# Transposing attention exponentials by DMA as two float16 values, in a kernel of attention, an FFN and a soft mixture of experts

## The chip, the cores and the metric

The kernel runs on one core of a Trainium2 chip. The metric is the device time of one execution in microseconds (us). The engines are PE (TensorE, which multiplies matrices), DVE (VectorE), ACT (ScalarE), POOL (GpSimd) and SP (SyncE, which here only issues DMAs). Each engine runs its own instructions in the order in which they were written. PE writes its results to PSUM, and another engine must move them from there.

## The reference

```python
# attention: 4 batches, 8 heads, 576 tokens, head size 64
scores = q @ k.T / 8
thresh = max(scores) - tau
scores = where(scores >= thresh, scores, -1e9)
attn = exp(scores - max(scores)); attn /= attn.sum() + 1e-9
x = (attn @ v), heads side by side             # 2304 tokens x 512
# FFN
g = relu(x @ w_in)**2                          # 512 -> 2048
x = g @ w_out                                  # 2048 -> 512
# soft mixture of experts: 8 experts with 4 slots each
logits = x @ phi
d = softmax(logits, over tokens); slot_input = d.T @ x
slot_out[e] = relu(slot_input[e] @ w1[e]) @ w2[e]
out = softmax(logits, over slots) @ slot_out
```

All is float32.

## The kernel before, in words

**Attention.** A job is a pair of heads of one batch; there are 16 pairs. A pair has five query tiles. Tiles j = 0 to 3 hold 128 queries of both heads; tile 4 ("mixed") holds the last 64 queries of each head. For each tile PE computes the scores into three PSUM banks (`s_mm`). For each head DVE scales them and takes the row maximum (`top`, line 442), POOL adds tau to that (`bound`, 448), ACT takes the exponentials (`expo`, 455), and DVE zeroes those under the threshold and sums the rest (`keep`, 459). The result e of a tile has 128 rows and 2 x 576 columns. The product with v contracts over keys, so e has to be transposed: PE does it in nine blocks of 128 x 128 (`turn`; the transposes stand under the helper's line 239), and ACT copies them out of PSUM into the tile pt (`evac`, 496 and 498).

**Groups.** Tiles 0 and 1 form group 0, tiles 2 and 3 group 1, and tile 4 group 2. Once a group's two tiles are transposed, PE multiplies v with pt (`av`: line 547 for each head, writing one half of the output's partitions, and 536 for the last 64 keys of both heads), and DVE multiplies by the reciprocal sums and writes the FFN's input xp (560). So an xp tile holds a unit of 256 tokens: one batch and one group, of all four head pairs. There are three buffers of xp.

**FFN and experts.** Nine units of 256 tokens go through the FFN. Its float32 products are split into high and low parts in the format float32r, three one-pass products each: 192 products for a unit (line 830). Before that, 32 chunks of weights are converted (`conv_ops`). w_out is folded into phi, so the logits come from the FFN's hidden layer (645). The end (`tail`) loads the expert weights into the buffers that come free.

**What sets the order.** A planner (`Plan`) simulates the engines at build time with a cost, a key (priority) and dependences for each step, and emits the instructions in the order that it finds. The engines then keep that order. Attention steps have keys by job, FFN steps on PE have keys behind all of them (`FKEY`), so that the FFN's products fill the gaps. Buffers are slots of a tag: `acq` takes one, `rel` gives it back. SP's DMAs share one modelled bus; the figure `dma=` is what a transfer holds it. A negative one (`turn`) also keeps SP busy until shortly before the transfer's end.

```python
self.bus = max(self.bus, self.now + DMA_LEAD) + o.dma
o.end = max(self.bus, o.end + DMA_LEAD) + DMA_TAIL
if o.turn:
    self.free[o.eng] = max(self.now + o.cost, self.bus - DMA_TAIL)
```

Of the kernel before, what the change touches and what calls it, by code (L numbers as in the profile page):

```python
# [9 lines left out]
F32 = mybir.dt.float32  # L10
F32R = mybir.dt.float32r
F16 = mybir.dt.float16
# [127 lines left out]
def tile_kernel(  # L140
# [34 lines left out]
    EB = 3  # L175
# [1 line left out]
    PTB = 2  # L177
    XPB = 3
    MMB = 4
    QKB = 3  # L180
    WAIT = 0.0
    DQ = 2.212
    T0 = 20.0
# [16 lines left out]
    state = {}  # L200
    plan = Plan(
        dict(
            s=1, ma=1, mm=MMB, u=UB, e=EB, em=1, pt=PTB, ptm=1, rp=3, rb=3, rr=3, xp=XPB, xh=2, xl=1, gt=MC // 2 + 1,
            gk=GB, l4=1, dT=1, qt=QKB, kt=QKB, vraw=2, vbd=2,
            sm=5, raw64=RB, cv=CB, wt=2,
        ),
        ("mm", "ma"),
        WAIT,
        DQ,
    )  # L210
# [1 line left out]
    def add(kind, eng, cost, fn, deps=(), key=0.0, *args, **kw):  # L212
        return plan.add(eng, cost, fn, deps, key + LEAD.get(kind, 0.0), *args, **kw)
# [6 lines left out]
    stack_f = const.tile([128, 128], F32, name="stack_f")  # L220
    stack_i = stack_f[:, 0:NS]
    tau_sb = const.tile([128, 1], F32, name="tau_sb")
    tau_p = const.tile([128, 1], F32, name="tau_p")
    nscale = const.tile([128, 1], F32, name="nscale")
    wphi = const.tile([128, MC, NS], F32, name="wphi")
# [14 lines left out]

    def setup():
        make_identity(nc, sg[:, 0:128])
        nc.vector.tensor_copy(ident_r, sg[:, 0:128])
        nc.sync.dma_start(out=tau_sb, in_=tau.partition_broadcast(128))
        nc.vector.tensor_scalar(tau_p, tau_sb, 0.0, None, ALU.max)
        nc.vector.tensor_scalar(nscale, tau_sb, 0.0, -SCALE, ALU.is_ge, ALU.mult)
        nc.vector.tensor_reduce(stack_i, ident.rearrange("p (g s) -> p s g", s=NS), AX.X, ALU.add)
        for g in range(1, NG):
            nc.vector.tensor_copy(stack_f[:, NS * g:NS * g + NS], stack_i)
# [100 lines left out]
    def attn_ops():  # L350

        at, ac = state["at"], state["ac"]
        vbd = [ac.tile([128, NP, 192], F32, name=f"vbd{i}") for i in range(2)]
        for t in vbd:
# [10 lines left out]

        def key(p, x):
            return begins[p] + x  # L370

        def prep(x):
            p, b, n, h0 = x, jobs[x][0] // NP, jobs[x][0] % NP, 2 * (jobs[x][0] % NP)
            d = P[x]
            k0 = key(x - 1, 2.0) if x else 0.0
            ld = {}
            if n == 0 and b not in last:
                def lvrem():
                    y = v[b, :, 512:S, :].rearrange("(n h) p d -> p n h d", h=2)
                    for a, r0, c0 in ((0, 0, 0), (1, 64, 64), (1, 0, 128)):  # L380
                        nc.sync.dma_start(out=vbd[b % 2][r0:r0 + 64, :, c0:c0 + 64], in_=y[:, :, a, :])
                last[b] = add("lrem", "SP", 1.9, lvrem, [], k0 - 4, ["vbd"], dma=1.1)
            for nm in "kqv":
                def lraw(nm=nm):
                    if nm == "v":
                        t = raw[p, nm] = at.tile([128, 2, 4 * D], F32, tag=nm + "raw", name="raw", bufs=2)
                        nc.sync.dma_start(
                            out=t, in_=v[b, h0:h0 + 2, 0:512, :].rearrange("h (r j) d -> r h (j d)", j=4)
                        )
                        return  # L390
                    t = d[nm + "t"] = at.tile([128, SQ], F32, tag=nm + "t", name=nm + "t", bufs=QKB)
                    nc.sync.dma_start(out=t, in_=src[nm][b, n])
                ld[nm] = add("lraw", "SP", 0.6, lraw, [], k0 - (5 if nm != "v" else 2), [nm + ("raw" if nm == "v" else "t")],
                             dma=0.73 if nm == "v" else 0.95)
            d["v_op"], d["vr_op"], d["q_op"], d["k_op"] = ld["v"], last[b], ld["q"], ld["k"]
            d["v"], d["vb"] = (lambda: raw[p, "v"]), vbd[b % 2][:, n, :]
            d["ready"] = [ld["q"], ld["k"]]

        def tiles(p):
            d = P[p]  # L400
# [4 lines left out]
            def tile_ops(n, j):  # L405
# [27 lines left out]
                for a in heads:  # L433
                    c = 0 if mixed else 2 * a + j % 2
                    k = key(p, n * TA + a * TA / 2)

                    def top(a=a, c=c):
                        if "sm" not in gd:
                            gd["sm"] = at.tile([128, 16], F32, tag="sm", name="sm", bufs=5)
                        u = o["u", a] = at.tile([128, S], F32, tag="u", name="u", bufs=UB)  # L440
                        s0 = 960 * a
                        nc.vector.tensor_scalar(  # L442
                            u, o["s"][:, s0:s0 + S], nscale, None, ALU.mult, ALU.min, accum_out=gd["sm"][:, c:c + 1]
                        )

                    def bound(c=c):
                        sm = gd["sm"]
                        nc.gpsimd.tensor_scalar(sm[:, 4 + c:5 + c], sm[:, c:c + 1], tau_p, None, ALU.add)  # L448

                    def expo(a=a, c=c):  # L450
                        if "e" not in o:
                            w = S if mixed else 2 * S
                            o["e"] = at.tile([128, w], F32, tag="em" if mixed else "e", name="e", bufs=1 if mixed else EB)
                        e = o["e"][:, a * S:(a + 1) * S]
                        nc.scalar.activation(e, o["u", a], AF.Exp, scale=-1.0, bias=gd["sm"][:, c:c + 1])  # L455

                    def keep(a=a, c=c):
                        sm, e = gd["sm"], o["e"][:, a * S:(a + 1) * S]
                        nc.vector.scalar_tensor_tensor(  # L459
                            e, o["u", a], sm[:, 4 + c:5 + c], e, ALU.is_le, ALU.mult, accum_out=sm[:, 8 + c:9 + c]  # L460
                        )

                    X = add("top", "DVE", 0.89, top, [S_], k, ["u"] + (["sm"] if first_g and not a else []), [("s", S_)])
                    if first_g and not a:
                        gd["first"] = X
                    h = add("bound", "POOL", 0.52, bound, [X], k)
                    E_ = add("expo", "ACT", 0.77, expo, [X] + ([ee] if a else []), k, [] if a else ["em" if mixed else "e"])
                    if not a:
                        ee = E_
                    K_ = add("keep", "DVE", 0.92, keep, [E_, h], k, rel=[("u", X)])  # L470
                    gd.setdefault("keep", []).append(K_)
                    ks.append(K_)

                def turn(x):
                    o["p", x] = mm_tile()
# [10 lines left out]

                def evac(x):
                    if "pt" not in gd:
                        w = 1 if mixed else 2
                        gd["pt"] = at.tile(  # L490
                            [128, 5 if mixed else 9, w, 128], F32, tag="ptm" if mixed else "pt", name="pt", bufs=1 if mixed else PTB
                        )
                    pt, i = gd["pt"], 0 if mixed else j % 2
                    if x == 2:
                        r, m = (slice(0, 64), 4) if mixed else (slice(0, 128), 8)
# [1 line left out]
                    else:  # L497
                        nc.scalar.activation(pt[:, 4 * x:4 * x + 4, i], o["p", x].rearrange("p (c s) -> p c s", c=4), AF.Copy)  # L498

                tag = "em" if mixed else "e"  # L500
                pk = "ptm" if mixed else "pt"
                for x in heads + (2,):
                    k = key(p, n * TA + min(x, 1) * TA / 2)
                    dep = ks if x == 2 else [ks[x]]
# [6 lines left out]
            def group_ops(g, n):  # L511
# [17 lines left out]
                def av(lo, hi):  # L529
# [4 lines left out]
                    for m in range(lo, hi):  # L534
# [5 lines left out]
                        for a in range(2):  # L540
# [4 lines left out]
                            else:  # L545
                                lt, rh = vr[:, a, m * D:(m + 1) * D], pt[:, 4 * a + m].rearrange("p t s -> p (t s)")
                            nc.tensor.matmul(po[i, :n_], lt, rh, start=m == 0, stop=m == 4)  # L547
                def evac():
                    if g == 2:
                        for a in range(2):  # L550
# [5 lines left out]
                    else:  # L556
                        if kk == 0:
                            xp[b, g] = fx.tile([128, KC, NU], F32, tag="xp", name="xp", bufs=XPB)
                        o = xp[b, g][:, kk, :]
                    nc.vector.tensor_tensor(o, gd["po"][:, 0:256], gd["rr"], ALU.mult)  # L560

                if g < 2:
                    rc = add("spread", "POOL", 0.6, spread, [rc], k, ["rb"], [("rp", rc)])
# [5 lines left out]
                        transpose(gd["ro"][:, 128 * t:128 * t + 128], y)  # L569

                def revac():
                    gd["rr"] = at.tile([128, 256], F32, tag="rr", name="rr", bufs=3)
                    n = 128 if g == 2 else 256
                    nc.scalar.activation(gd["rr"][:, 0:n], gd["ro"][:, 0:n], AF.Copy)

# [2 lines left out]
                rc = add("r_evac", "ACT", 0.3 if g == 2 else 0.4, revac, [rt], k, [], [("mm", rt)])  # L578
                deps = gd["turn"] + [d["v_op"], d["vr_op"]]
                first = None  # L580
                for lo, hi_ in ((0, 5),) if g == 2 else ((0, 2), (2, 5)):
                    c = (hi_ - lo) * (0.51 if g < 2 else 0.3) 
                    rel = []
                    if hi_ == 5:
                        rel = [("ptm" if g == 2 else "pt", gd["pto"])]
                    o = add("av", "PE", c, lambda lo=lo, hi_=hi_: av(lo, hi_), deps, k, [] if lo else ["ma"], rel)
                    first = first or o
                    deps = [o]
                rel = [("ma", first), ("rr", rt)]
                ev = add("evac", "DVE", 0.25 if g == 2 else 0.45, evac, [o, rc], k, ["xp"] if g < 2 and kk == 0 else [], rel)  # L590
                ev_at.setdefault("rem" if g == 2 else (b, g), []).append(ev)
                att.append(ev)
# [548 lines left out]
```

## Time and profile before

| What | Value |
|---|---|
| Median of 3 runs | 738.61 us (738.5 to 738.76) |
| The profiled execution's own time | 741.05 us |
| Its span, first to last instruction | 739.2 us |
| Busy: PE, DVE, ACT, POOL | 674.4, 423.7, 373.4, 133.6 us |
| Mean granted TensorE clock | 0.974 of full speed |
| Attention's writes of xp | from 41.0 us to 503.6 us |
| FFN products | from 159.0 us to 661 us |

A row of a group of instructions reads: line, engine, operation, tile written <- tiles read, shape, count | busy us together, mean ns of one | idle time of the engine just ahead of them and what ended it. The mean of a matmul is its latency: matmuls are pipelined, so what one takes from PE is the distance to the next one's start. A timeline row gives start, length, engine, line, and how many equal instructions were merged. A row of DMA issues ends with the KB of one and the us from issue to landing. PEld is PE's weight load, SPq is SP's queue.

### The profile page before, as it was taken

How to read it: one execution, taken by the hardware profiler on the slowest of the kernel's cores; microseconds unless marked ns; L12 is line 12 of the kernel's file. 1: busy time of each engine (PE TensorE's matmuls, PEld its weight loads, DVE VectorE, ACT ScalarE, POOL GpSimd, SP SyncE). 2: the span in 40 equal slices, each digit the busy share in tenths (PEclk: the TensorE clock that was granted, in tenths of full speed). 3: DMA queues.
4: the chain of work that ended last, by engine and by line, in shares of the span. 5: the costliest groups of instructions: out<-in, count | busy, mean ns of one | idle time of the engine just before them, and what ended most of it. 6: DMA issues, size and time to landing. Idle time of an engine off the chain costs nothing.

```text
span 739.2 us, 13383 instructions
## 1 busy us (share of the span) xinstructions
PE 674.4 (91%) x5198; PEld 489.8 (66%) x5198; DVE 423.7 (57%) x1110; ACT 373.4 (51%) x726; POOL 133.6 (18%) x236
## 2 busy tenths in 40 slices
PE   1677899999999999999999999999999999998873
PEld 0333666767676766877678769767988979794312
DVE  6999978876677668746677571572323140413403
ACT  4776766765666556537566543654333333332203
POOL 4876433210211111111012100010000000000000
PEclk9888979999999999999999999999999999999998
DMA  7955857311110210010110000105900000197986
GB/s 229 305 167 178 264 166 247 110 45 51 36 52 16 61 37 4 34 51 30 47 36 6 1 1 1 30 1 184 397 4 30 1 30 1 59 367 277 388 319 255
DMA packets 38959, 83.50 MB, mean 113 GB/s; under 512 B 6641, under 2 KB 11761, under 8 KB 38897
## 3 DMA queue, kind: packets, MB, share of 16 engines
q1 hardware_dynamic: 38896, 82.65, 32.8%
q8 instruction: 41, 0.67, 0.4%
q14 instruction: 22, 0.17, 0.1%
HBM read 73.73 MB, written 8.91 MB: 112 GB/s over the span
## 4 chain that ended last, share of the span: by engine, by line
PE 79%; DVE 8%; DMA 4%; ACT 4%; issue 2%; POOL 1%; SPq 1%; DVEq 0%; ACTq 0%; POOLq 0%
PE mm L830 29%; PE mm L239 16%; PE po L547 9%; PE s L426 8%; PE mm L759 2%; PE mm L645 2%; PE po L536 2%; DMA w<-in_moe_w_dram 2%; PE mm L961 2%; PE s L421 2%; DVE raw L286 1%; PE s L415 1%; DVE cv L290 1%; DVE e L459 1%; PE mm L332 1%
## 5 line engine op out<-in xcount | busy, mean ns | idle before, releaser
L830 PE MATMUL mm<-xh,w 128*128 128x256 f32 x1152 | 166.4, 287 | 0.0
L830 PEld LDWEIGHTS mm<-xh,w 128*128 128x128 f32 x1152 | 147.6, 191 | 13.7 <-issue 11.0
L459 DVE SCALAR_TENSOR_TENSOR e<-u,sm,e 128x576 f32<-128x576 f32 x144 | 122.7, 862 | 35.0 <-ACT e L455 32.9
L442 DVE TENSOR_SCALAR_CACHE_REDUCE u<-s,nscale 128x576 f32<-128x576 f32 x144 | 114.5, 811 | 49.2 <-PE s L426 40.9
L455 ACT ACTIVATE e<-u,sm 128x576 f32<-128x576 f32 x144 | 110.0, 779 | 32.1 <-DVE u L442 31.4
L498 ACT ACTIVATE pt<-mm 128x512 f32<-128x512 f32 x144 | 82.8, 597 | 55.1 <-PE mm L239 54.8
L836 ACT ACTIVATE gt<-mm 128x512 f32<-128x512 f32 x72 | 43.0, 597 | 125.8 <-PE mm L830 124.8
L448 POOL TENSOR_SCALAR sm<-sm,tau_p 128x1 f32<-128x1 f32 x144 | 53.1, 369 | 287.9 <-DVE u L442 228.9
L239 PE MATMUL mm<-ident_r,e 128*128 128x128 f32 (+1 forms) x656 | 98.0, 286 | 5.6 <-DVE e L459 5.6
L239 PEld LDWEIGHTS mm<-ident_r,e 128*128 128x128 f32 (+1 forms) x656 | 76.5, 146 | 33.4 <-DVE e L459 12.6
L830 PE MATMUL mm<-xl,w 128*128 128x256 f32 x576 | 92.5, 283 | 0.0
L547 PE MATMUL po<-pt,raw 128*64 128x256 f32 (+1 forms) x768 | 79.0, 342 | 0.9 <-DVE xp L560 0.9
L830 PEld LDWEIGHTS mm<-xl,w 128*128 128x128 f32 x576 | 79.3, 192 | 0.0
L426 PE MATMUL s<-kt,qt 64*128 64x512 f32 x256 | 77.0, 680 | 0.0
L547 PEld LDWEIGHTS po<-pt,raw 128*64 128x64 f32 x768 | 44.6, 140 | 29.2 <-issue 10.7
L421 PE MATMUL s<-kt,qt 128*128 128x128 f32 x128 | 27.3, 297 | 29.4 <-DMA qt<-in_q_dram 11.9
L842 DVE SCALAR_TENSOR_TENSOR gt<-mm,gt 128x512 f32<-128x512 f32 x18 | 12.4, 691 | 67.7 <-ACT gt L836 67.5
L421 PEld LDWEIGHTS s<-kt,qt 128*128 128x128 f32 x128 | 20.7, 201 | 33.7 <-issue 19.8
L239 PEld LDWEIGHTS mm<-ident_r,gt 128*128 128x128 f32 x288 | 31.7, 143 | 11.2 <-issue 8.2
L239 PE MATMUL mm<-ident_r,gt 128*128 128x128 f32 x288 | 38.7, 278 | 0.3 <-ACT pt L498 0.2
L844 ACT ACTIVATE gt<-gt 128x512 f32<-128x512 f32 x54 | 34.0, 630 | 1.4
L801 POOL TENSOR_TENSOR xl<-xp,xh 128x256 fp32r<-128x256 f32 x16 | 12.3, 780 | 115.9 <-PE mm L830 82.6
(126 smaller groups left out, 742.0 us busy)
## 6 DMA issues: line engine op xcount, KB each, us to landing
w<-in_moe_w_dram SPq DMA_DIRECT2D x25, 1024.0 KB, 11.9
raw<-in_moe_w_in_dram SPq DMA_DIRECT2D x16, 512.0 KB, 4.4
raw<-in_moe_w_out_dram SPq DMA_DIRECT2D x16, 512.0 KB, 4.2
kt<-in_k_dram SPq DMA_DIRECT2D x20, 320.0 KB, 3.1
qt<-in_q_dram SPq DMA_DIRECT2D x20, 320.0 KB, 4.0
raw<-in_v_dram SPq DMA_DIRECT2D x20, 256.0 KB, 2.8
w_out<-cv SPq DMA_DIRECT2D x16, 256.0 KB, 4.8
w<-w_out SPq DMA_DIRECT2D x4, 1024.0 KB, 9.8
```

What stands on the lines that cost most here:

```text
L239: nc.tensor.transpose(out_, in_, ident[:n, :n])
L421: nc.tensor.matmul(s[:, 1].rearrange("p (c s) -> p c s", s=64)[:, 0:8:7], lt, d["kt"][:, 512:SQ], start=True, stop=True)
L426: nc.tensor.matmul(s[:, 2 * a], lt[i], d["kt"][i, 0:512], start=True, stop=True)
L442: nc.vector.tensor_scalar(u, o["s"][:, s0:s0 + S], nscale, None, ALU.mult, ALU.min, accum_out=gd["sm"][:, c:c + 1])
L448: nc.gpsimd.tensor_scalar(sm[:, 4 + c:5 + c], sm[:, c:c + 1], tau_p, None, ALU.add)
L455: nc.scalar.activation(e, o["u", a], AF.Exp, scale=-1.0, bias=gd["sm"][:, c:c + 1])
L459: nc.vector.scalar_tensor_tensor(e, o["u", a], sm[:, 4 + c:5 + c], e, ALU.is_le, ALU.mult, accum_out=sm[:, 8 + c:9 + c])
L498: nc.scalar.activation(pt[:, 4 * x:4 * x + 4, i], o["p", x].rearrange("p (c s) -> p c s", c=4), AF.Copy)
L547: nc.tensor.matmul(po[i, :n_], lt, rh, start=m == 0, stop=m == 4)
L830: nc.tensor.matmul(o["h"][:, i * NU:(i + 1) * NU], a, c, start=n_ == 0, stop=n_ == len(terms) - 1)
L836: nc.scalar.activation(g, o["h"], AF.Relu)
L844: nc.scalar.activation(g, g, AF.Square)
```

## The change

For 18 groups (in batches 2 to 4: group 1 of every head pair, and group 0 of every second one) the transposes leave PE:

- e is split into two float16 values, a high part (ACT, `high`) and the remainder (POOL, `low`), side by side in a tile hl of 128 x 2304.
- One DMA from SP (`dturn`) transposes that tile from SBUF to SBUF, 18 blocks of 128 x 128. PE's transposes and ACT's evacuations of these tiles go.
- v is also split into two float16 parts, once for each head pair that has such a group (`split_v`). A power of two scales v into range; it comes from the sum of absolute values (two ACT passes with a sum, two one-column PE products, four short DVE steps). Then ACT makes the high part and DVE the low one.
- The product becomes three one-pass float16 products (`av_split`): high with high, low v with high e, and high v with low e. The scale is undone when DVE writes xp.
- For space: k and q have two buffers instead of three, rr two instead of three, and the mixed tiles take their e and pt buffers from the common ones. The planner hands out xp slots to whichever step comes first.

```diff
-    QKB = 3
+    QKB = 2
+    HB = 2
...
-            s=1, ma=1, mm=MMB, u=UB, e=EB, em=1, pt=PTB, ptm=1, rp=3, rb=3, rr=3, xp=XPB, xh=2, xl=1, gt=MC // 2 + 1,
+            s=1, ma=1, mm=MMB, u=UB, e=EB, pt=PTB, rp=3, rb=3, rr=2, hl=HB, vh=1, mx=2, xp=XPB, xh=2, xl=1, gt=MC // 2 + 1,
...
-        ("mm", "ma"),
+        ("mm", "ma", "xp"),
...
+        def by_dma(p, g):
+            b, n = jobs[p][0] // NP, jobs[p][0] % NP
+            return g < 2 and (b > 0 and (g == 1 or n % 2 == 1))
...
+        def split_v(x):
+            p, d, k0 = x, P[x], key(x, 0.0)
+            def absum():
+                mx = d["mx"] = at.tile([128, 16], F32, tag="mx", name="mx", bufs=2)
+                d["vh"] = at.tile([128, 2, 640], F16, tag="vh", name="vh", bufs=1)
+                main = d["v"]().rearrange("p h d -> p (h d)")
+                nc.scalar.activation(d["vh"][:, 0, 0:512], main, AF.Abs, accum_out=mx[:, 0:1])
+                nc.scalar.activation(d["vh"][:, 1, 0:128], d["vb"][:, 0:128], AF.Abs, accum_out=mx[:, 1:2])
+            def stats():
+                d["ps"] = mm_tile()
+                for i in range(2):
+                    nc.tensor.matmul(
+                        d["ps"][:, 0:1], ones.to_broadcast([128, 128]), d["mx"][:, i:i + 1], start=i == 0, stop=i == 1
+                    )
+            def scales():
...
+            def hi():
+                for t, y in parts():
+                    nc.scalar.activation(t[:, 0], y, AF.Copy, scale=d["mx"][:, 8:9])
+            def lo():
+                for t, y in parts():
+                    nc.vector.scalar_tensor_tensor(t[:, 1], y, d["mx"][:, 8:9], t[:, 0], ALU.mult, ALU.subtract)
+            ab = add("v_abs", "ACT", 0.9, absum, [d["v_op"], d["vr_op"]], k0, ["mx", "vh"])
+            st = add("v_sum", "PE", 0.4, stats, [ab], k0, ["mm"])
+            sc = add("v_scale", "DVE", 0.5, scales, [st], k0, rel=[("mm", st)])
+            h = add("v_hi", "ACT", 0.9, hi, [sc], k0)
+            d["vs_op"], d["vs_ready"] = ab, add("v_lo", "DVE", 0.95, lo, [h], k0)
...
+                def high(a):
+                    if not a:
+                        o["hl"] = at.tile([128, 4 * S], F16, tag="hl", name="hl", bufs=HB)
+                    nc.scalar.activation(o["hl"][:, a * S:(a + 1) * S], o["e"][:, a * S:(a + 1) * S], AF.Copy)
+                def low(a):
+                    c = slice(a * S, (a + 1) * S)
+                    nc.gpsimd.tensor_tensor(
+                        o["hl"][:, (2 + a) * S:(3 + a) * S], o["e"][:, c], o["hl"][:, c], ALU.subtract
+                    )
+                def dturn():
+                    if "pt" not in gd:
+                        gd["pt"] = at.tile([128, 2, 18, 128], F16, tag="pt", name="pt", bufs=PTB)
+                    nc.sync.dma_start_transpose(out=gd["pt"][:, j % 2], in_=o["hl"])
+                if by_dma(p, g) and not mixed:
+                    ls = []
+                    for a in heads:
+                        k = key(p, n * TA + a * TA / 2)
+                        h = add("high", "ACT", 0.68, lambda a=a: high(a), [ks[a]] + ([hl] if a else []), k, [] if a else ["hl"])
+                        hl = hl if a else h
+                        ls.append(add("low", "POOL", 1.72, lambda a=a: low(a), [h], k, rel=[("e", ee)]))
+                    k = key(p, n * TA + TA / 2)
+                    t = add("dturn", "SP", 3.0, dturn, ls, k, [] if "pto" in gd else ["pt"], [("hl", hl)], dma=-6.8)
+                    gd.setdefault("pto", t)
+                    gd.setdefault("turn", []).append(t)
+                    return
...
+                def av_split():
+                    po = gd["po"] = ma.tile([128, 512], F32, tag="ma", name="po", bufs=1)
+                    terms = ((0, 0), (1, 0), (0, 9))
+                    for i, (y, c) in enumerate(terms):
+                        for m in range(4):
+                            for a in range(2):
+                                c0 = 256 * a + m * D
+                                nc.tensor.matmul(
+                                    po[64 * a:64 * a + 64, :n_], d["vh"][:, y, c0:c0 + D], gd["pt"][:, :, c + 5 * a + m, :],
+                                    start=i == 0 and m == 0, stop=False,
+                                )
+                    for i, (y, c) in enumerate(terms):
+                        nc.tensor.matmul(
+                            po[:, :n_], d["vh"][:, y, 512:640], gd["pt"][:, :, c + 4, :], start=False, stop=i == 2
+                        )
...
+                if by_dma(p, g):
+                    o = first = add("av", "PE", 1.9, av_split, deps + [d["vs_ready"]], k, ["ma"],
+                                    [("pt", gd["pto"]), ("vh", d["vs_op"])])
```

More of the change, by code (lines that the diff above doesn't have):

```diff
@@ L222, in tile_kernel @@
     tau_sb = const.tile([128, 1], F32, name="tau_sb")
+    ones = const.tile([128, 1], F32, name="ones")
     tau_p = const.tile([128, 1], F32, name="tau_p")
@@ L242, in setup @@
         make_identity(nc, sg[:, 0:128])
+        nc.vector.memset(ones, 1.0)
         nc.vector.tensor_copy(ident_r, sg[:, 0:128])
@@ L397, in prep, with parts @@
             d["ready"] = [ld["q"], ld["k"]]
+            if any(by_dma(x, j // 2) for j in jobs[x][1] if j < 4):
+                split_v(x)
+        def split_v(x):
[13 more added lines that the diff above has]
+            def scales():
+                mx = d["mx"]
+                e, f = mx[:, 4:5], mx[:, 8:9]
+                nc.vector.tensor_scalar(e, d["ps"][:, 0:1], 2.0**-40, None, ALU.max)
+                nc.vector.tensor_scalar(e.bitcast(I32), e.bitcast(I32), 0x7F800000, None, ALU.bitwise_and)
+                nc.vector.tensor_scalar(f.bitcast(I32), e.bitcast(I32), -1.0, 268.0 * 2**23, ALU.mult, ALU.add)
+                nc.vector.tensor_scalar(mx[:, 12:13], e, 2.0**-14, None, ALU.mult)
+            def parts():
+                v = d["v"]().rearrange("p h d -> p (h d)")
+                return (d["vh"][:, :, 0:512], v), (d["vh"][:, :, 512:640], d["vb"][:, 0:128])
+            def hi():
[9 more added lines that the diff above has]
+            d["vs_op"], d["vs_ready"] = ab, add("v_lo", "DVE", 0.95, lo, [h], k0)
+            plan.release(d["vs_ready"], [("vraw", d["v_op"]), ("vbd", d["vr_op"])])
@@ L451, in expo @@
                         if "e" not in o:
-                            w = S if mixed else 2 * S
-                            o["e"] = at.tile([128, w], F32, tag="em" if mixed else "e", name="e", bufs=1 if mixed else EB)
+                            o["e"] = at.tile([128, 2 * S], F32, tag="e", name="e", bufs=EB)
                         e = o["e"][:, a * S:(a + 1) * S]
@@ L466, in tile_ops @@
                     h = add("bound", "POOL", 0.52, bound, [X], k)
-                    E_ = add("expo", "ACT", 0.77, expo, [X] + ([ee] if a else []), k, [] if a else ["em" if mixed else "e"])
+                    E_ = add("expo", "ACT", 0.77, expo, [X] + ([ee] if a else []), k, [] if a else ["e"])
                     if not a:
@@ L488, in evac @@
                     if "pt" not in gd:
[L489 to L492, printed above, removed]
+                        gd["pt"] = at.tile([128, 9, 2, 128], F32, tag="pt", name="pt", bufs=PTB)
                     pt, i = gd["pt"], 0 if mixed else j % 2
@@ L498, in evac @@
                         nc.scalar.activation(pt[:, 4 * x:4 * x + 4, i], o["p", x].rearrange("p (c s) -> p c s", c=4), AF.Copy)
-                tag = "em" if mixed else "e"
-                pk = "ptm" if mixed else "pt"
+                tag, pk = "e", "pt"
                 for x in heads + (2,):
@@ L559, in evac @@
                         o = xp[b, g][:, kk, :]
-                    nc.vector.tensor_tensor(o, gd["po"][:, 0:256], gd["rr"], ALU.mult)
+                    if by_dma(p, g):
+                        nc.vector.scalar_tensor_tensor(o, gd["po"][:, 0:256], d["mx"][:, 12:13], gd["rr"], ALU.mult, ALU.mult)
+                    else:
+                        nc.vector.tensor_tensor(o, gd["po"][:, 0:256], gd["rr"], ALU.mult)
                 if g < 2:
@@ L571, in revac @@
                 def revac():
-                    gd["rr"] = at.tile([128, 256], F32, tag="rr", name="rr", bufs=3)
+                    gd["rr"] = at.tile([128, 256], F32, tag="rr", name="rr", bufs=2)
                     n = 128 if g == 2 else 256
@@ L580, in group_ops @@
                 first = None
-                for lo, hi_ in ((0, 5),) if g == 2 else ((0, 2), (2, 5)):
+                if by_dma(p, g):
+                    o = first = add("av", "PE", 1.9, av_split, deps + [d["vs_ready"]], k, ["ma"],
+                                    [("pt", gd["pto"]), ("vh", d["vs_op"])])
+                for lo, hi_ in () if by_dma(p, g) else ((0, 5),) if g == 2 else ((0, 2), (2, 5)):
                     c = (hi_ - lo) * (0.51 if g < 2 else 0.3)
@@ L584, in group_ops @@
                     if hi_ == 5:
-                        rel = [("ptm" if g == 2 else "pt", gd["pto"])]
+                        rel = [("pt", gd["pto"])]
                     o = add("av", "PE", c, lambda lo=lo, hi_=hi_: av(lo, hi_), deps, k, [] if lo else ["ma"], rel)
@@ L588, in group_ops @@
                     deps = [o]
-                rel = [("ma", first), ("rr", rt)]
+                rel = [("ma", first), ("rr", rt)] + ([("mx", d["vs_op"])] if by_dma(p, g) else [])
                 ev = add("evac", "DVE", 0.25 if g == 2 else 0.45, evac, [o, rc], k, ["xp"] if g < 2 and kk == 0 else [], rel)
```

## The prediction

> **What bounds the kernel now.** First the page's busy shares and slices, then busy times by stretch.
>
> ```profile
> PE 674.4 (91%) x5198; PEld 489.8 (66%) x5198; DVE 423.7 (57%) x1110; ACT 373.4 (51%) x726; POOL 133.6 (18%) x236
> PE   1677899999999999999999999999999999998873
> ```
> ```profile
> 20.00:80.00 60.00, 43.67 (x208) 26.01 (x210) 59.37 (x117) 41.97 (x78) 42.15 (x43) 0.83 0.69 222
> 140.00:500.00 360.00, 356.58 (x2782) 258.97 (x2782) 232.95 (x668) 205.80 (x414) 52.47 (x144) 1.00 0.10 31
> ...
> 506.00:661.00 155.00, 153.60 (x1318) 137.55 (x1319) 40.06 (x102) 56.34 (x105) 5.74 (x8) 1.00 0.32 118
> 661.00:740.00 79.00, 56.72 (x453) 24.14 (x451) 24.50 (x66) 16.31 (x33) 1.90 (x2) 0.95 0.84 309
> ```
>
> The columns are window, length, then busy us of PE, its weight loads, DVE, ACT, POOL, then granted clock, DMA share, GB/s. From 20 to 80 us DVE is the bound (59.4 of 60). From 140 to 661 PE is (356.6 of 360, then 153.6 of 155); DVE is at 65% there, DMA at 0.10. The end after 661 is set by weight loads (DMA 0.84). So time taken from PE between 140 and 500, where batches 2 to 4 run their attention, shortens the kernel as long as PE finds other work. That other work is the FFN: the attention's writes to the xp tiles show how both are tied.
>
> ```profile
> 154.00 0.42 DVE L560 TENSOR_TENSOR xp<-po,rr 128x256 f32<-128x256 f32 x1 [0.24 <-PE po L536]
> ...
> 261.08 0.42 DVE L560 TENSOR_TENSOR xp<-po,rr 128x256 f32<-128x256 f32 x1
> ...
> 324.30 0.28 DVE L795 CAST xh<-xp 128x256 fp32r<-128x256 f32 x1
> 324.50 0.41 DVE L560 TENSOR_TENSOR xp<-po,rr 128x256 f32<-128x256 f32 x1
> ...
> 417.96 0.28 DVE L795 CAST xh<-xp 128x256 fp32r<-128x256 f32 x1
> 418.16 0.41 DVE L560 TENSOR_TENSOR xp<-po,rr 128x256 f32<-128x256 f32 x1
> ...
> 503.57 0.42 DVE L560 TENSOR_TENSOR xp<-po,rr 128x256 f32<-128x256 f32 x1 [1.91 <-PE po L536]
> ```
>
> Between 261 and 324 no attention output is written: the first one of batch 3's second unit comes right behind the read (L795) that frees an xp tile, and so again at 418. The attention waits for FFN units, and FFN for PE. Faster PE therefore also moves the attention forward.
>
> **The change part by part.** A "group" is two 128-row tiles of a head pair; 18 groups, 36 tiles, take the new path.
>
> ```profile
> 250.03 1.20 PE L239 MATMUL mm<-ident_r,e 128*128 128x128 f32 x9
> ...
> 250.99 1.19 PE L830 MATMUL mm<-xh,w 128*128 128x256 f32 x8
> ...
> 257.76 1.95 PE L547 MATMUL po<-pt,raw 128*64 128x256 f32 x16
> ...
> 259.64 0.70 PE L536 MATMUL po<-pt,vbd 128*128 128x256 f32 x2
> ...
> 260.18 0.38 PE L239 MATMUL mm<-ident_r,rb 128*128 128x128 f32 x2
> ```
> ```profile
> 443.13 17.46 PE mm L830 x144
> ```
> ```profile
> L704 PE MATMUL mm<-al,stack_f 32*128 32x1 f32 x16 | 2.9, 250 | 0.0
> ```
>
> *Removed from PE.* Nine transposes of a tile hold PE from 250.03 to 250.99, the next start: 0.96 us. Two tiles: 1.92 us per group. The float32 product with v lasts from 257.76 to 260.18: 2.42 us. Together 4.34.
>
> *Added to PE.* 27 products of 256 columns: 24 write half of the output's partitions and 3 write all. No float16 product is in the trace. The nearest row is the FFN's one-pass product of the same 256 columns, 17.46/144 = 0.121 us. If the two heads' products run side by side, as the float32 ones do (16 records, two for each of 8 products, in 1.88 us: 0.47 for a pair, near four passes of 0.121), there are 12 + 3 slots: 1.82 us. If they don't, 27 slots: 3.27 us. I take 1.82, since the float32 rows show the pairing. Saved: 2.52 us per group, 45.4 us in 18; low end 1.07 per group, 19 us.
>
> The sum over v's partitions adds two one-column products for each of 12 head pairs. L704's 16 records are eight products, 2.9/8 = 0.36 us each; 24 of them cost 8.7 us. PE net: 45.4 - 8.7 = 36.7 us (ends 10.6, and 45.4 if the sums fall into gaps).
>
> ```profile
> L459 DVE SCALAR_TENSOR_TENSOR e<-u,sm,e 128x576 f32<-128x576 f32 x111 | 89.6, 817 | 31.9 <-ACT e L455 30.1 <-POOL sm L448 1.2
> ...
> L498 ACT ACTIVATE pt<-mm 128x512 f32<-128x512 f32 x112 | 64.3, 598 | 43.4 <-PE mm L239 43.2
> ...
> L844 ACT ACTIVATE gt<-gt 128x512 f32<-128x512 f32 x24 | 15.1, 628 | 0.5
> ...
> L496 ACT ACTIVATE pt<-mm 128x128 f32<-128x128 f32 x50 | 14.1, 281 | 5.6 <-PE mm L239 5.6
> ```
> ```profile
> L299 POOL TENSOR_TENSOR cv<-cv,raw 128x512 f32<-128x512 f32 x16 | 23.8, 1488 | 18.9 <-DVE cv L290 9.1 <-ACT raw L294 5.2 <-DMA raw<-in_moe_w_out_dram 3.5
> ```
> ```profile
> L459 DVE SCALAR_TENSOR_TENSOR e<-u,sm,e 128x576 f32<-128x576 f32 x16 | 17.2, 1085 | 0.5 <-ACT e L455 0.5
> ```
>
> *ACT.* Evacuations go: 36 x (2 x 0.598 + 0.281) = 53 us. The float16 halves come: 72 x 0.628 x 576/512 = 51 us; v's magnitude and high part, 12 x 2 x (0.628 + 0.281) = 22 us. 206 becomes 226 of some 345 us (the 360 less part of the gain): beside PE.
>
> *POOL.* The low halves are 72 x 1.488 x 576/512 = 121 us, so POOL goes from 52 to 173 us. It isn't full, but its other steps (L448, which L459 waits for) queue behind a 1.67 us instruction.
>
> *DVE.* v's low parts, 12 x 0.817 x 640/576 = 11 us; four one-column steps for each pair at about 0.2, 10 us. And L459 takes 1085 ns in 20 to 80 us, where POOL is busy for 70%, against 817 where it is for 15%. At about 50% I put 0.17 us on each of 111: 19 us. DVE: 233 + 40 = 273 of 345 us, 79%; below the 99% of 20 to 80, where PE got only 43.7 of 60. The Trainium skill, "GPSIMD Engine Reference", Specifications, says that POOL shares its SBUF interfaces with VectorE and contends with two-input instructions; the two L459 rows agree.
>
> *The transposes.* 36 DMAs of 128 x 2304 float16, 576 KB each, on SP's queue. None is in the trace.
>
> ```profile
> raw<-in_moe_w_in_dram SPq DMA_DIRECT2D x16, 512.0 KB, 4.4
> ...
> kt<-in_k_dram SPq DMA_DIRECT2D x20, 320.0 KB, 3.1
> ...
> vbd<-in_v_dram SPq DMA_DIRECT2D x12, 64.0 KB, 3.1
> ```
>
> Lower end: a plain load of this size, 4.4 us x 576/512 = 5.0 us. Upper end: the rate of the small-run vbd rows, 9 x 3.1 = 28 us. The kernel's own plan books 6.8 us of the DMA engines for one and keeps SP for as long. Its other bookings are near their rows (0.59 for L498's 0.598, 1.31 for twelve FFN products of 1.45), so I take 6.8, which lies near the lower end. Per batch, 12 x 6.8 = 82 us; SP's loads wait behind, 4 x about 2.6 us by the plan's bookings (0.95 + 0.95 + 0.73): 92 us.
>
> ```profile
> 529.54 2.04 PE mm L645 x32
> 562.54 2.04 PE mm L645 x32
> ```
> ```profile
> L830 PE MATMUL mm<-xh,w x1152: 274/283/388, 159.0 to 660.7; 128*128 128x256 f32 x192
> ```
> ```profile
> 264.00 1.21 PE L830 MATMUL mm<-xh,w 128*128 128x256 f32 x8
> ```
> ```profile
> 154.00:244.00 90.00, 89.69 (x673) 62.71 (x672) 63.19 (x180) 55.48 (x111) 14.61 (x42) 1.00 0.16 44
> ```
>
> The cover: an FFN unit alone takes PE 33 us (562.54 - 529.54). Batch 2's outputs fall in 154 to 244, 90 us of full PE. The first FFN unit's products run beside them from 159.0 until the second unit's start at 264.00, so about 85/105 of its 33 us, 27, lie in these 90. Attention alone is thus 63 us, after the change 63 - 6 x 2.52 + 4 x 0.72 = 51. With two FFN units that are ready, PE has 51 + 66 = 117 us of work per batch against 92 of DMA. The cover is gone at (117 - 10)/12 = 8.9 us for a transpose; from there each further us costs 36.
>
> The Trainium skill is of two minds on this price. "VectorE: DVE Perf Modes", The three transpose paths, lists 1309 ns for a 128x128 16-bit block by DMA; 18 blocks would be an estimate of 23.6 us. "Advanced Engine Details and Errata", X-Bar Transpose (TRN2), calls them as fast as ordinary DMAs, which by the 4.4 us row is 5.0. No run here shows which holds.
>
> *Buffers.* k and q tiles go from 3 to 2, rr from 3 to 2, and the mixed tiles now share e and pt. Before 140 us DVE is the bound and loads come ahead; I cost this at nothing, covered by DVE's queue, and -2 to +5 us if the cover goes. The end after 661 moves as a block.
>
> *Late steps.* PE's order is fixed at build time, so a product that waits for a late transpose holds the FFN behind it. The path keep, high, low, transpose is some 0.7 + 1.7 + 8.9 us where it was 1.6. I charge 18 groups x 0.25 us = 4.5 us; ends 0 and 18 x 1.5 = 27.
>
> The sum: the profiled execution took 741.05 us with a span of 739.2; 741.05 - 36.7 + 4.5 = 708.9. The median of the runs is 2.4 us lower, 738.6, so 706.
>
> **The rivals.**
> 1. *Transposes too slow.* SP's queue becomes the bound. For: 2-byte items, and the vbd rows show small runs at a seventh of the rate of 512 KB loads. Against: the same queue is idle for 90% between 140 and 500. At 10 us: 706 + 36 x 1.1 = 746, slower; at 13 us 854; at the vbd rate's 28 us, 1394. It decides from 9.8 us on, where 0.9 x 36 = 32 us eat the gain. Its chance is 0.20, of which 0.04 for rates near the upper end. By the 1309 ns of the skill's page named above the time would be 706 + 36 x (23.6 - 8.9) = 1235, inside that 0.04.
> 2. *POOL and DVE become the bound.* For: 20 to 80 us, where POOL at 70% leaves PE starved by 16 of 60 us. Against: 79% of DVE. If a tenth of 345 us is so lost, the late steps' 4.5 within it, 706 + 34.5 - 4.5 = 736, with the edge beyond 739.
> 3. *More than counted.* The sums of v fall into gaps and no product is late: 706 - 8.7 - 4.5 = 693.
> 4. *Products not paired.* 706 + 26 = 732.
>
> **How the numbers follow.** Forecast, 695 to 724 around 706: 0.57. Rival 1: 0.20, about a quarter of it below 755 (transposes up to 10.2 us). Rival 2: 0.10 (faster 0.05, same 0.02, slower 0.03). Rival 3: 0.06. Rival 4: 0.07. A measurement here tells 0.2%, 1.5 us, from no change. Faster: 0.57 + 0.05 + 0.06 + 0.07 = 0.75, less 0.01 for rival 4's edge, 0.74; same 0.03; slower 0.23. From 688 to 755 only most of rival 1 and bits of the others are out, under 0.2.
>
> **What would show it.** Right: the transposes land in about 9 us, 7 apart; PE stays above 97% between 140 and the last xp write; the group's products take 1.8 to 2.0 us; L459 is near 1.0 us; FFN units alone still 33 us. Wrong: PE waits for DMA ahead of the products, transposes over 9 us apart (rival 1); DVE above 90% with PE waits for it (2); products at 3.3 us (4).

## The result, and the profile after

The changed kernel takes 696.5 us (694.9 to 698.5) against 738.6 before; the ratio is 0.940, 95% interval 0.9365 to 0.9438. Predicted were 706 us, and 695 to 724 for the likeliest case. The changed kernel was measured again together with the runs of 12 groups, 24 groups and three transposes: 700.4 us and 0.945 (0.9412 to 0.9487). The other experiments ran in two further sets, each with its own runs of the kernel before (739.3 and 740.0 us), so experiments are compared within a set or by their ratio. The traces of the two measurements differ by 5.8 us, and 4.4 us of that lie ahead of the first new product (at 188.8 and 193.2 us), where the granted clock between 80 and 140 us was 0.97 and 0.89: some 4 us between two traces say nothing of the change itself.

The page of the changed kernel, busy shares:

```profile
PE 630.1 (91%) x5084; PEld 458.4 (66%) x5084; DVE 456.8 (66%) x1183; ACT 393.2 (57%) x762; POOL 233.1 (34%) x308
```

Busy times by stretch, columns as before:

```profile
140.00:500.00 360.00, 354.35 (x3000) 266.13 (x3000) 271.70 (x752) 238.02 (x472) 148.04 (x211) 1.00 0.43 87
...
500.00:620.00 120.00, 118.98 (x1066) 104.71 (x1067) 35.38 (x94) 46.89 (x90) 12.05 (x14) 1.00 0.50 170
617.00:695.00 78.00, 58.96 (x461) 25.37 (x459) 24.51 (x66) 16.33 (x33) 1.90 (x2) 0.94 0.84 318
```

PE's busy time fell by 674.4 - 630.1 = 44.3 us, the span by 739.2 - 694.8 = 44.4. PE is still full from 140 us to the end of the FFN (354.4 of 360, then 119.0 of 120), and the end of the program still takes 78 us. So the gain is PE's work. The medians give 42.1 us, and 39.2 in the second measurement, so up to 5 us were given back.

PE's timeline around one group's product and one sum over v:

```profile
248.61 1.50 PE L635 MATMUL po<-pt,vh 128*64 128x256 f16 x24
250.04 0.50 PE L640 MATMUL po<-pt,vh 128*128 128x256 f16 x3
250.30 0.96 PE L932 MATMUL mm<-xh,w 128*128 128x256 f32 x6
```
```profile
251.81 0.50 PE L424 MATMUL mm<-mx,ones 128*128 128x1 f32 x4
...
252.17 0.47 PE L477 MATMUL s<-kt,qt 128*128 128x128 f32 x2
```

This group's product lasts from 248.61 to the next start at 250.30: 1.69 us where it was 2.42. It is one of the three shortest: the 18 take 1.69 to 1.87 us, median 1.77, 32.3 together, depending on what follows. A pair's sums hold PE from 251.81 to 252.17, 0.36 us; all twelve take 4.7. Summed over both whole traces, from each start to the next, PE has 35.6 us less of transposes of e and 12.3 less of products with v (12.8 in the expectations below), and 4.7 more of sums: 43.2 net, near the 44.4.

The DMA transposes, with min, median and max of their issue on SP in ns, and their time to landing:

```profile
L543 SPq DMA_TRANSPOSE pt<-hl x36: 2457/2705/3585, 168.7 to 517.9; - x36
...
DMA to landing us min/median/max: 4.5/4.6/6.3
```

They land after 4.6 us. Predicted were 8.9, and the lowest row that the prediction named gave 5.0.

Groups of the other engines in 140 to 500 us:

```profile
L514 DVE SCALAR_TENSOR_TENSOR e<-u,sm,e 128x576 f32<-128x576 f32 x108 | 90.6, 856 | 21.9 <-ACT e L510 19.0 <-POOL sm L504 2.2 <-issue 0.4
L536 POOL TENSOR_TENSOR hl<-e,hl 128x576 f16<-128x576 f32 x68 | 90.2, 1337 | 82.0 <-ACT hl L532 67.5 <-issue 14.1 <-POOL xl L903 0.2
```

POOL's subtraction takes 1.34 us instead of 1.67, and DVE's step beside it 856 ns instead of about 990. DVE is busy 272 us of 360, 75%.

The writes of attention outputs (first and last start) on the new path:

```profile
L657 DVE SCALAR_TENSOR_TENSOR xp<-po,mx,rr x18: 475/484/485, 190.8 to 531.2; 128x256 f32<-128x256 f32 x18
```

The last one starts at 531.2; before, it was at 503.57. The attention ends 28 us later and the kernel is 44 us shorter: the saved PE time went to FFN units. Behind the last attention output 157 us of FFN were left before, 86 now. The kernel with another booking, below, shows that the later end costs nothing.

### The profile page after: what moved, and what is told of

The parts are those of the page before. It is cut to its first block, busy times and chain, and to the rows that moved or that the text cites. A ratio compares the mean times of both kernels' runs of the same rounds, so it can differ in the third digit from the quotient of the medians.

```text
span 694.8 us, 13413 instructions
## 1 busy us (share of the span) xinstructions
PE 630.1 (91%) x5084; PEld 458.4 (66%) x5084; DVE 456.8 (66%) x1183; ACT 393.2 (57%) x762; POOL 233.1 (34%) x308
## 4 chain that ended last, share of the span: by engine, by line
PE 74%; DVE 10%; DMA 5%; ACT 4%; issue 4%; POOL 1%; SPq 0%; DVEq 0%; POOLq 0%; ACTq 0%
PE mm L932 30%; PE mm L241 11%; PE s L482 8%; PE po L627 4%; DVE e L514 3%; PE po L635 3%; PE mm L861 2%; PE mm L747 2%; PE mm L1063 2%; DMA w<-in_moe_w_dram 2%; PE s L477 2%; DMA w_out<-cv 2%; PE s L471 2%; DVE cv L293 2%; ACT e L510 1%
## 5 line engine op out<-in xcount | busy, mean ns | idle before, releaser
L514 DVE SCALAR_TENSOR_TENSOR e<-u,sm,e 128x576 f32<-128x576 f32 x144 | 125.4, 885 | 26.1 <-ACT e L510 22.9
L536 POOL TENSOR_TENSOR hl<-e,hl 128x576 f16<-128x576 f32 x72 | 95.5, 1337 | 84.6 <-ACT hl L532 69.9
L504 POOL TENSOR_SCALAR sm<-sm,tau_p 128x1 f32<-128x1 f32 x144 | 60.7, 424 | 141.1 <-DVE u L498 108.9
L241 PE MATMUL mm<-ident_r,e 128*128 128x128 f32 (+1 forms) x332 | 53.3, 296 | 6.0 <-DVE e L514 5.2
L241 PEld LDWEIGHTS mm<-ident_r,e 128*128 128x128 f32 (+1 forms) x332 | 39.9, 151 | 26.8 <-issue 10.0
L532 ACT ACTIVATE hl<-e 128x576 f16<-128x576 f32 x72 | 48.1, 679 | 11.8 <-DVE e L514 11.5
L579 ACT ACTIVATE pt<-mm 128x512 f32<-128x512 f32 x72 | 41.7, 594 | 21.9 <-PE mm L241 21.6
L627 PE MATMUL po<-pt,raw 128*64 128x64 f32 (+1 forms) x480 | 42.0, 309 | 0.0
L241 PEld LDWEIGHTS mm<-ident_r,gt 128*128 128x128 f32 x288 | 31.5, 142 | 12.1 <-issue 8.2
```

What stands on the lines that cost most here:

```text
L241: nc.tensor.transpose(out_, in_, ident[:n, :n])
L514: nc.vector.scalar_tensor_tensor(e, o["u", a], sm[:, 4 + c:5 + c], e, ALU.is_le, ALU.mult, accum_out=sm[:, 8 + c:9 + c])
L532: nc.scalar.activation(o["hl"][:, a * S:(a + 1) * S], o["e"][:, a * S:(a + 1) * S], AF.Copy)
L536: nc.gpsimd.tensor_tensor(o["hl"][:, (2 + a) * S:(3 + a) * S], o["e"][:, c], o["hl"][:, c], ALU.subtract)
```

## The experiments

In the expectations, 35.7, 12.8 and 4.7 us (transposes, products, sums) are sums of the distances from one matmul's start to the next over both traces of the first comparison. All kernels are edits of the changed one.

**Only the buffers and the order.**

```diff
-            return g < 2 and (b > 0 and (g == 1 or n % 2 == 1))
+            return False
```

> The changed kernel with the new path switched off for every group: only the smaller and shared buffers and the freely handed out xp slots are left. Theory (the gain is PE's saved time): no PE work is saved, so about the time of before, 735 to 742 us. Rival (part of the gain, or a hidden loss, lies in the buffers and in the planner's new order): more than 4 us away from 738.6 on either side.

744.2 us, ratio 1.0044 (1.002 to 1.0069). PE is as full as before (140 to 500 us):

```profile
140.00:500.00 360.00, 355.10 (x2753) 255.37 (x2752) 226.58 (x651) 202.05 (x404) 50.23 (x138) 1.00 0.11 33
```

The buffers given up and the new order cost 0.2 to 0.7%, about 3 us by the ratio. That is inside the theory's range; the median itself, 744.2, lies in the rival's, so the two aren't told apart. None of the gain comes from here: it had to make up for this too, and 43.2 less 3 lies between the 39 and 42 us by which the medians fell. Which of the edits (k and q, rr, common e and pt, free xp slots) costs it was not tried.

**The products alone, transposes on PE.** ACT writes the high part from PSUM; DVE takes the low one from PSUM.

```diff
+                def plow(x):
+                    nc.vector.tensor_tensor(part(x, 1)[0], part(x, 0)[1], part(x, 0)[0], ALU.subtract)
...
+                        nc.scalar.activation(*part(x, 0), AF.Copy)
...
-                if by_dma(p, g) and not mixed:
+                if False:
```

> The 18 groups keep their transposes on PE in float32; ACT copies the high float16 part out of PSUM, DVE takes the low part from PSUM (36 x 1.6 us more on DVE, POOL's 72 subtractions and the DMA transposes go). Products, split v and scale as in the changed kernel. Theory (PE's time decides): products save 12.8 us of PE and the sums cost 4.7, so 738.6 - 8 = 730 us (726 to 734), and the other 35 us of the gain are the transposes'. Rival (DVE becomes the bound at 300 of 350 us): 738 or more.

746.6 us, ratio 1.0085 (1.0054 to 1.0115), so no gain over the kernel with the buffers alone. Busy times in 140 to 500 us, and PE's longest wait there (total us, number, longest):

```profile
140.00:500.00 360.00, 350.20 (x2934) 263.40 (x2933) 283.96 (x810) 222.09 (x473) 54.10 (x136) 0.99 0.11 33
```
```profile
PE s L477 <- DVE u L498: 3.2, 4, 1.2
```

The theory's 730 fell. PE is idle for 9.8 of the 360 us where it was for 4.9 with the buffers alone. The two longest waits there, 3.2 us in four and 1.8 us in one, are ended by DVE, whose busy time rose from 227 to 284 us. So the rival's engine does hold PE up now and then, without being full; that DVE is the bound isn't shown. These waits are not the whole loss, and where the rest of the 8 us went is open. In the changed kernel neither ACT nor DVE copies these tiles out of PSUM, so the two halves of the change can't be priced apart by adding.

**The transposes twice and three times.** The order of all engines' other instructions stays.

```diff
                     nc.sync.dma_start_transpose(out=gd["pt"][:, j % 2], in_=o["hl"])
+                    nc.sync.dma_start_transpose(out=gd["pt"][:, j % 2], in_=o["hl"])
```

> Each DMA transpose is issued twice into the same tile, in the same order of instructions: a tile's transpose takes about 9.2 instead of 4.6 us. Theory of the prediction (PE has other work up to 8.9 us for a transpose): 697 to 712 us. Rival (the fixed order makes PE wait for each late tile): 18 groups by one or two times 4.6 us, 740 to 860 us.

> Each DMA transpose three times into the same tile, same order: 13.9 us for a tile. Theory of the prediction (PE has other work up to 8.9 us, then each us costs 36): 697 + 36 x 5.0 = 877 us. Rival (attention can run far enough ahead, the cover is wider): under 800 us.

Twice: 705.7 us (699.5 to 709.1), ratio 0.951 (0.9445 to 0.9584). Three times: 859.0, ratio 1.161 (1.159 to 1.163). PE's waits for a transposed tile, first with two, then with three (total us, number, longest):

```profile
PE po L636 <- DMA pt<-hl: 3.6, 3, 1.7
```
```profile
PE po L637 <- DMA pt<-hl: 116.8, 18, 11.6
```

The copies run one behind the other. From a tile's first issue to its last it takes 5.3 us with two and 10.1 with three, on average over the 36 tiles; with 4.6 for the last landing a tile takes some 9.9 and 14.7 us, a little more than the 9.2 and 13.9 of the expectations. At 9.9 us PE hardly waits for a transpose (3.6 us in three waits), and the 5 us above the changed kernel's 700.4 lie within the spread (the intervals overlap). The 4.8 us more for each of 36 tiles then cost 153 us, 32 for each us. So there is an edge and a price near the predicted 36 beyond it. With only one point beyond the edge the two can't be separated: at 36 for each us the edge lies at 14.7 - 158.6/36 = 10.3 us, not at 8.9. The formula's 877 came near 859 in part because the tile was taken as 13.9 us; with 14.7 it gives 906. The waits stand ahead of the 18 products, while the same 86 to 88 us of FFN are left behind the attention as in the changed kernel: with transposes this late the fixed order does hold the FFN back.

**v scaled by a constant.** The sums of magnitudes, their products on PE and the short DVE steps are left out; v is multiplied by a fixed 1024.

```diff
-            ab = add("v_abs", "ACT", 0.9, absum, [d["v_op"], d["vr_op"]], k0, ["mx", "vh"])
-            st = add("v_sum", "PE", 0.4, stats, [ab], k0, ["mm"])
-            sc = add("v_scale", "DVE", 0.5, scales, [st], k0, rel=[("mm", st)])
+            ab = sc = add("v_scale", "DVE", 0.2, scales, [d["v_op"], d["vr_op"]], k0, ["mx", "vh"])
```

> v is scaled by a fixed 1024 instead of a power of two from its sum of magnitudes: both ACT passes with a sum, the 24 one-column products on PE and the four short DVE steps of each pair go (two memsets stand in their place). Theory (PE's time decides): the 48 product records held PE for 4.7 us between starts, so 696.5 - 4.7 = 692 us. The prediction's own price, 8.7 us: 688 us. Rival (the sums lie in gaps of PE): 696 us.

702.4 us, ratio 0.948 (0.944 to 0.952), against the theory's 692: no better than the changed kernel's 0.940 and 0.945. Busy times from 160 to 610 us, the changed kernel first, then this one:

```profile
160.00:610.00 450.00, 443.33 (x3792) 346.00 (x3789) 292.27 (x799) 266.50 (x524) 156.33 (x216) 1.00 0.44 103
```
```profile
160.00:610.00 450.00, 437.90 (x3710) 340.86 (x3710) 288.80 (x774) 253.17 (x478) 160.07 (x216) 0.99 0.42 97
```

PE is idle for 12.1 instead of 6.7 us: waits in the planner's other order took back what the sums had cost. So there is no gain, as the rival expected, but not for its reason: in the trace above the sums stand between other products on a full PE. See the last experiment.

**The changed kernel again.**

> The changed kernel once more, as the reference for the other runs of this set: 696 us if this chip gives the same as the first, and 0.938 to 0.944 of the kernel before. If the fixed-scale kernel's 702 us were a loss by its order, this one stays near 697; if it was this chip, this one shows 700 to 707.

700.4 us, 0.945: inside the range that was expected if the difference lay with this chip. The fixed scale's 702.4 is thus neither a loss nor a gain that can be told from it.

**Twelve groups and 24 groups.**

```diff
-            return g < 2 and (b > 0 and (g == 1 or n % 2 == 1))
+            return g == 1 and b > 0          # 12 groups
...
+            return g < 2 and b > 0           # 24 groups
```

> Only group 1 of every head pair on the new path: 12 groups, 24 transposes, all 12 splits of v. Theory: 6 x 2.7 = 16 us more than the changed kernel, about 713. If the gain per group fell with the number of groups (a limit is near): less than 8 us more, under 705.

> All 24 groups of batches 2 to 4 on the new path (48 transposes, no further split of v). Theory (PE's time decides): transposes 35.7 us and products 12.8 us fewer in 18 groups is 2.7 us a group, so 16 us less than the changed kernel, about 681. Rival (DMA and SP: the plan books 48 x 6.8 = 326 us of the stretch's 350, and its order becomes the transposes'): 696 or more. Rival (POOL and DVE at their limit): between 685 and 696.

Twelve: 718.2 us, ratio 0.9713 (0.9685 to 0.974), 17.8 above 18 groups, so 3.0 us a group and the theory's 2.7 nearly met. From no group (744.2, in another set) to twelve it is 26 us, 2.2 a group with the sums of all twelve pairs in it, 2.5 without their 4.7. Twenty-four: 714.4 us, ratio 0.9658 (0.9638 to 0.9677). Here six groups more cost 14 us, as the rival with the plan's booking expected. Its transposes and its busy times:

```profile
L543 SPq DMA_TRANSPOSE pt<-hl x48: 2432/2702/4787, 158.4 to 544.0; - x48
```
```profile
140.00:540.00 400.00, 374.83 (x3155) 278.78 (x3155) 294.67 (x788) 248.13 (x485) 191.24 (x242) 0.98 0.49 97
```

PE stands idle for 25 of 400 us, though neither DMA (0.49) nor DVE (295) is full. The transposes come at (544.0 - 158.4)/47 = 8.2 us from one to the next, much more than they take, and close to the 6.8 us that the plan books plus its loads.

**The plan's booking.** Only the order changes.

```diff
-                    t = add("dturn", "SP", 3.0, dturn, ls, k, [] if "pto" in gd else ["pt"], [("hl", hl)], dma=-6.8)
+                    t = add("dturn", "SP", 3.0, dturn, ls, k, [] if "pto" in gd else ["pt"], [("hl", hl)], dma=-2.6)
```

> The changed kernel (18 groups) with the plan's booking of a transpose changed from 6.8 to 2.6 us, so that its landing in the plan, 1.13 + 2.6 + 0.95 = 4.7 us, and SP's 3.0 us agree with the measured 4.6 and 2.7. Nothing but the order changes. Theory A (in the changed kernel PE is full, the booking only decides when a transpose is issued): 693 to 701 us. Theory B (the booked 6.8 us hold the attention back and cost PE time already with 18 groups): 685 to 692.

> All 24 groups with the booking of 2.6 us. Theory (the 24 groups at 714 us lost to the booked pace of some 8 us for a transpose, which stretched the attention to 548 us and left PE without FFN units): the loss goes and 6 x 2.7 us come on top of the changed kernel, 681 to 690 us. Rival (POOL with 96 subtractions, or the chain of keep, high, low and transpose itself, is the limit with 24 groups): 700 to 715 us as before the change of booking.

> All 24 groups, booking 4.0 us: a landing of 6.1 us in the plan, later than measured. Theory of the booking: between 681 and 714, nearer the lower end (48 x some 5.2 us are 250 of 350 us, no longer the plan's bound), 682 to 695. Rival: 700 or more.

> All 24 groups, booking 2.6 us, and v scaled by the fixed 1024 (no sums of magnitudes). If the sums' 4.7 us on PE are on the path: 4 to 5 us below the same kernel with the sums. If an order with them is as good because they fill gaps, as with 18 groups: no less than 2 us below it.

| Kernel | Median, us | Ratio to the kernel before, 95% interval |
|---|---|---|
| 18 groups, booking 6.8 (the change) | 696.5; 700.4 | 0.940 (0.9365 to 0.9438); 0.945 (0.9412 to 0.9487) |
| 18 groups, booking 2.6 | 701.5 | 0.948 (0.942 to 0.954) |
| 24 groups, booking 6.8 | 714.4 | 0.966 (0.964 to 0.968) |
| 24 groups, booking 4.0 | 692.5 | 0.938 (0.932 to 0.944) |
| 24 groups, booking 2.6 | 692.8 | 0.936 (0.932 to 0.939) |
| 24 groups, booking 2.6, fixed scale | 685.8 | 0.928 (0.924 to 0.932) |

The 24 groups' transposes and busy times with a booking of 2.6:

```profile
L543 SPq DMA_TRANSPOSE pt<-hl x48: 2438/2707/4668, 160.0 to 515.0; - x48
```
```profile
140.00:540.00 400.00, 388.49 (x3356) 297.23 (x3355) 310.19 (x804) 257.88 (x498) 198.12 (x244) 0.98 0.53 111
```

The same work in another order ends its transposes at 515 instead of 544, leaves PE idle for 11.5 instead of 25 us, and is 22 us faster. A booking of 4.0 gives the same 692.5. So these 22 us were the booking's, and not a limit of DMA, SP, POOL or DVE. With 18 groups the booking makes no difference (701.5 against 700.4; 701.5 is at the upper edge of theory A's range), as theory A expected: PE is full either way. The attention does end earlier with it:

```profile
L657 DVE SCALAR_TENSOR_TENSOR xp<-po,mx,rr x18: 466/482/485, 186.5 to 495.8; 128x256 f32<-128x256 f32 x18
```

The last output starts at 495.8 instead of 531.2, and the time is the same: with PE full, the attention's end did not decide here. Of the 16 us that six more groups should bring, 8 to 9 are there (692.8 against 701.5 in the same set), so 681 to 690 was missed and the rival's 700 to 715 as well; the rest isn't settled. PE's 11.5 us of idle time are part of it, and DVE is at 310 of 400 us, near the rival's limit but not at it.

On this kernel the fixed scale gives 7 us by the medians and 5.5 by the ratios (the intervals touch at 0.932), a little over the 4 to 5 expected. That fits sums that lie on PE's path and, with 18 groups, another order that hid it. It isn't proven: this edit changes the order too, and no run held the order fixed. The fixed scale holds only for values of v that 1024 keeps inside float16's range, unlike the scale from the sums; 24 groups with a booking of 2.6 is the version without that condition, and it beats the changed kernel by 1% of the time at the second measurement's ratio (0.936 against 0.945), by less at the first's (0.940, intervals overlapping).

## Why the prediction was right, point by point

- *PE is the bound and the FFN fills it*: right. PE stays at 98% between 140 and 500, FFN units alone still take 33.0 us, no wait of PE for a transpose stands among its waits from 140 to 620, and the span fell by what PE saved.
- *Removed and added on PE*: 36.7 us were predicted, 43.2 measured. The product was put at 1.82 us a group and took 1.79 on average, so the two heads' products pair and the unpaired case fell. The largest miss is the sums, 8.7 us against 4.7: the 0.36 us taken from L704 is the busy time of a product that stands alone, latency included, while here two products follow each other in 0.36 us from start to start.
- *Late steps*: charged with 4.5 us; the changed kernel loses nearly nothing there. The mechanism exists (116.8 us of waits with three transposes), its size at 4.6 us for a transpose was over-estimated.
- *Buffers at nothing*: measured 0.2 to 0.7% (1.5 to 5 us), inside the -2 to +5.
- *The sum*: 6.5 us of PE and 4.5 of late steps make the forecast too long, the buffers' 3 too short. That leaves 698, and 696.5 and 700.4 were measured. The range held because the misses are small; that the buffers' cost offset part of the others is luck.
- *The transposes' price*: 8.9 us to landing were taken from the plan's booking, 4.6 measured, under the lower end of the range. The step that failed is "so I take 6.8", the plan's booking of a transpose trusted because its other bookings are near their rows. It cost the forecast of the time little, as both lie under the edge of the cover. (The vbd rows, read there as a seventh of the rate of 512 KB loads, are nearer a sixth.) Of the two statements weighed from the Trainium skill, that of "Advanced Engine Details and Errata", X-Bar Transpose (TRN2), stands: 576 KB transposed land in 4.6 us, beside 4.3 for a plain 512 KB load in the same trace. The 1309 ns for one block in the Trainium skill's "VectorE: DVE Perf Modes", The three transpose paths, can't be added up: 18 blocks took 4.6 us, not 23.6.
- *The cover*: two and three transposes confirm that there is an edge with a steep price beyond it. The edge is nearer 10.3 us than 8.9 if the price is 36. Rival 1 is thus a true mechanism whose condition wasn't met. One of its signs did show: the transposes start (517.9 - 168.7)/35 = 10.0 us apart on average, not 7. The queue isn't full then (one lands in 4.6 us of these 10), and PE doesn't wait for them.
- *DVE, ACT, POOL*: over the whole kernel DVE's busy time rose by 33 us (predicted 40), ACT's by 20 (20), POOL's by 100 (121). The step beside POOL slowed to 856 ns, not to 990, and the four short steps of each pair take 7 us together, not 10. Rival 2 didn't occur.
- *"Faster PE therefore also moves the attention forward"*: wrong here. The last output came 28 us later; with a booking of 2.6 it came 8 us earlier than before, in the same time. The forecast didn't rest on it.

## What to carry to other kernels

Where one engine is full and another stage's work can fill every gap, price a change by what it takes from that engine, start to start, and then ask at which latency of the new step the filler runs out. Here the first held to some 10 us of 740, the second to about 1.5 us of a transpose. When a kernel's order comes from a planner, a booked duration that is too long can do harm without any real limit: here it cost nothing with 36 transposes and 22 us with 48. Compare the booking with the landing time after the first run. A saving on the full engine may vanish in another order (the fixed scale with 18 groups), so try it again once the larger limit is gone.

## What the runs showed of the hardware

A DMA transpose of 128 x 2304 float16 from SBUF to SBUF lands after 4.6 us and holds SP's queue for 2.7 us, where the issue of a plain load of q, k or v takes 0.38 to 0.43 us at the median (0.33 to 1.12). Three times 36 of them, copies one behind the other beside the kernel's other traffic, kept 4.6 us as the median each. Float16 products of 256 columns into the two halves of the output's partitions run side by side: 24 of them took 250.04 - 248.61 = 1.43 us, 0.060 us each, half of the 0.121 that the FFN's full-width product of 256 columns takes. With 3 products to the full width a group took 1.69 to 1.87 us.
